# Row statistics ahead of the next projection, one root for four tiles, first weights on the sync queue

## The chip, the cores and the metric

The kernel runs on one core of a Trainium2 chip. A core has five engines that run side by side and are tied together by semaphores: TensorE (PE: matmuls, with PEld for its weight loads), VectorE (DVE), ScalarE (ACT), GpSimd (POOL) and SyncE (SP), which issues DMAs. ACT and POOL issue DMAs too. The metric is the time of one execution on the device, in microseconds (us); lower is better.

## The reference

A layer norm of x (2048 rows of 640) feeds an attention of 32 heads over cached keys and values and, beside it, a gated feed-forward network; the two outputs are multiplied and added to x.

```python
def _layernorm(x, axis=-1, eps=1e-5):
    m = jnp.mean(x, axis=axis, keepdims=True)
    v = jnp.var(x, axis=axis, keepdims=True)
    return (x - m) / jnp.sqrt(v + eps)
...
    def _A_ref(x, k_cache, v_cache, wq, wo):     # Sq = Sk = 2048, H = 32, Dh = 192
        q = (x @ wq).reshape(B, Sq, H, Dh).transpose(0, 2, 1, 3)
        scores = jnp.einsum("bhqd,bhkd->bhqk", q, k_cache) * (Dh ** -0.5)
        p = _softmax(scores, axis=-1)
        o = jnp.einsum("bhqk,bhkd->bhqd", p, v_cache)
        return o.transpose(0, 2, 1, 3).reshape(B, Sq, H * Dh) @ wo
    def _B_ref(x, w1, w3, w2):                   # F = 1536
        h = _silu(x @ w1) * (x @ w3)
        return h @ w2
    xn = _layernorm(x)
    return x + _A_ref(xn, ...) * _silu(_B_ref(xn, ...))
```

Here the transposes of the reference's lambda are written as method calls; the computation is the same.

## The kernel before

**Tiles and stages.** The 2048 rows of x are 16 tiles of 128 rows; four tiles make a query block (qb 0 to 3, 512 rows). The 2048 keys are 16 tiles, taken two at a time: a pair p, 0 to 7, is key tiles p and p + 8. A head is 4 query blocks of 8 pairs. The text writes (qb, p) for a step of head 0. After the heads come the rest of the feed-forward network and the output projection, which the change does not touch.

**A step.** `advance` (line 446) takes one step: `scores` (L374 to 387) does six half-array matmuls into a PSUM tile st2, `weights` (L391) exponentiates it on ScalarE with a bound `nb` as bias, into pT2, and `values` (L420 to 440) multiplies pT2 by the values vt into two output banks (obank, L431), in two halves of 8 matmuls. Halves are queued and done some steps later, so that TensorE has work while ScalarE exponentiates. At p = 7 `evict` (L394) adds and scales the banks on VectorE (L401 to L408). The PSUM pool ps_st has two buffers, which st2, the projections' ps and the transposes' pst share by turns.

**Projections.** `project_chunk` (L274) makes the queries of one head for one query block: matmuls of the transposed normalized rows xnT with the head's weights wq (L283 for head 0, L289 for the others, which also use xnS, a copy of xnT with its partition halves exchanged), two casts qA and qF (L291, L292; ScalarE or VectorE), and copies qS and qD by GpSimd (L295, L299). It hands back `maxima` (L303): the largest absolute values of qA and qF. With those of the keys (`key_maxima`, L315) and a sum over partitions (`bound` on GpSimd, L343; `first_bound` by a matmul, L330) they give `nb`. `finish_head` (L350) does this for a whole later head.

**Layer norm.** It is done in head 0, between the steps. `ln_stats(i)` takes mean and variance of tile i on VectorE (L184, L185); `ln_sums` does the same on ScalarE for tiles 1 and 4 (L190 to L192). `ln_root(i0)` turns two variances into two factors by a logarithm and an exponential on ScalarE (L203 to L211), and `ln_scale(i0)` scales two tiles on VectorE (L221). Tiles 0 to 7 are then turned by TensorE into a PSUM tile pst and copied to xnT (`ln_turn`, L225 to L232; `next_turn`, L234); tiles 8 to 15 are sent by transposing DMAs on SP (`ln_send`, L238, L241). `swap_rows(qb)` (L307) copies 512 columns of xnT to xnS with two DMAs issued by GpSimd.

**What sets the order.** `pin` keeps instructions in program order on their engine: nearly all of head 0 is written out by hand. The tables `posts` and `extra_at` (L493 to L516) say which layer-norm work and which projection follows or stands within which step; a step with an `extra` keeps one half of values more in the queue. A queue serves its instructions in order, so an exponential on ScalarE stands behind a root issued before it, and that root behind VectorE's statistics. At (2,2) and (3,5) the keys and the weights of head 2 are asked for. On SP the order at the start is:

```python
load_x(nc.sync, 0, 1); load_x(nc.sync, 2, 4)     # tile 1 goes on the ACT queue
# keys KA in two halves; x tiles 4 to 7; keys KB in two halves; values vt
# x tiles 8 to 11; x tiles 12 to 15
```

and the weights of head 0 go on the ACT queue (L95).

Of the kernel before, what the change touches and what calls it, by code (L numbers as in the profile page):

```python
# [16 lines left out]
P = 128  # L17
# [13 lines left out]
def _kernel_impl(ctx, tc, A_x, A_k_cache, A_v_cache, A_wq, A_wo, B_w1, B_w3, B_w2, out):  # L31
# [54 lines left out]
    def load_weights(h):  # L86
# [15 lines left out]
    def load_keys(h, mid=None):  # L102
# [5 lines left out]
        for K, c in ((KA, 0), (KB, DH - P)):  # L108
            for r in ((slice(0, HALF), slice(HALF, SK)) if h == 0 else (slice(0, SK),)):
                keep(nc.sync.dma_start_transpose(out=K[:, r], in_=kh[r, c:c + P]))  # L110
            if mid and K is KA:
                mid()
# [16 lines left out]
    with ExitStack() as actx:  # L129
# [26 lines left out]
        ASUM = {1: 0, 4: 1}  # L156
        sums = lnx.tile([P, 2], F32, name="sums")
        sqs = lnx.tile([P, 2], F32, name="sqs")
        nmean = lnx.tile([P, 2], F32, name="nmean")
# [27 lines left out]
        def ln_sums(i):  # L187
            k = slice(ASUM[i], ASUM[i] + 1)
            junk = lnp.tile([P, D], BF16, tag="junk", name="junk")
            pin(nc.scalar.activation(out=junk[:], in_=x_all[:, i, :], func=ACT.Identity, accum_out=sums[:, k]))  # L190
            pin(nc.scalar.mul(out=nmean[:, k], in_=sums[:, k], mul=-1.0 / D))
            pin(nc.scalar.activation(out=junk[:], in_=x_all[:, i, :], func=ACT.Square, bias=nmean[:, k], scale=1.0,  # L192
                                     accum_out=sqs[:, k]))
# [3 lines left out]
        def ln_root(i0):  # L197
            lv = lnp.tile([P, 2], F32, tag="lv", name="lv")
            if i0 in ASUM or i0 + 1 in ASUM:
                for t in range(2):  # L200
                    i = i0 + t
                    if i in ASUM:
                        pin(nc.scalar.activation(out=lv[:, t:t + 1], in_=sqs[:, ASUM[i]:ASUM[i] + 1], func=ACT.Ln, bias=eps_t[:],  # L203
                                                 scale=1.0 / D))
                    else:
                        pin(nc.scalar.activation(out=lv[:, t:t + 1], in_=mv[:, i, 1:2], func=ACT.Ln, bias=eps_t[:], scale=1.0))
            else:
                pin(nc.scalar.activation(out=lv[:].unsqueeze(2), in_=mv[:, i0:i0 + 2, 1:2], func=ACT.Ln, bias=eps_t[:],
                                         scale=1.0))
            rstd[i0] = lnx.tile([P, 2], F32, name=f"rstd{i0}")  # L210
            pin(nc.scalar.activation(out=rstd[i0][:], in_=lv[:], func=ACT.Exp, scale=-0.5))  # L211
# [3 lines left out]
        def ln_scale(i0):  # L215
            scaled[i0] = []
            for t in range(2):
                i = i0 + t
                xn = xnp.tile([P, D], BF16, tag="xn", name="xn")
                act = i in ASUM  # L220
                pin(nc.vector.tensor_scalar(out=xn[:], in0=x_all[:, i, :], scalar1=nmean[:, ASUM[i]:ASUM[i] + 1] if act else mv[:, i, 0:1],  # L221
                                            scalar2=rstd[i0][:, t:t + 1], op0=ALU.add if act else ALU.subtract, op1=ALU.mult))
# [22 lines left out]
        loads[0].update(load_weights(0))  # L245
# [7 lines left out]
        for copy in ln_turn(0):  # L253
            copy()
        keep_busy(2)
        for copy in ln_turn(2):
            copy()
        keep_busy(4)

# [14 lines left out]
        def project_chunk(h, qb, cast=nc.vector.tensor_copy):  # L274
# [17 lines left out]
            pin(cast(out=qF[:, qs], in_=ps[:, 512:1024]))  # L292
            keep = pin if h == 0 or h == 1 else (lambda x: x)
            for t in range(2):
                keep(nc.gpsimd.tensor_copy(out=qS[ROWS[t], qs], in_=qA[ROWS[1 - t], qs]))  # L295
            if h == 0 and qb == 0:
# [579 lines left out]
```

## Time and profile before

| | us |
|---|---|
| median of 3 runs | 1957.99 (1957.71 to 1958.47) |
| the profiled execution | 1959.34 |
| its span (first to last instruction) | 1957.3 |
| TensorE busy | 1937.9 (99%) |
| ScalarE busy | 1214.6 (62%) |
| VectorE busy | 1143.3 (58%) |
| GpSimd busy | 443.7 (23%) |

The profile page divides the span into 40 slices and gives the busy share of each engine in tenths. TensorE's row shows an 8 in the first slice and 9 from there to the last but one. Finer windows of the trace show where it is not busy: those from 0 to 100 us add up to 86.7 us of a busy TensorE, those from 100 to 300 us to 200.0.

How to read the lines: a group line gives source line, engine, operation and tiles, then total and mean duration. A waits line reads "engine line <- who ended the wait: total us, times, longest us". A timeline line begins with start and duration, and ends with the idle time in front of it and what ended it. A row of windows gives for each engine the busy time and in brackets the number of instructions, in the order PE, PEld, DVE, ACT, POOL; then the TensorE clock granted (1.00 is full), the busy share of the DMA engines and GB/s. "to landing" is the time from the issue of a DMA to its completion.

### The profile page before, as it was taken

The numbers are of one execution on the slowest core, as the hardware profiler recorded it, in microseconds if no ns is written. First come the engines' busy times: TensorE is split into PE (matmuls) and PEld (weight loads), VectorE is DVE, ScalarE is ACT, GpSimd is POOL, SyncE is SP. The second block draws the span as 40 slices with busy tenths as digits, with TensorE's granted clock in tenths as the row PEclk, the third lists the DMA queues.
The fourth block names the chain that finished last, engine by engine and source line by source line (L and its number), as shares of the span: only waits on it lengthen the run. The fifth ranks groups of instructions, "written<-read, shape, count | busy, mean of one in ns | idle before, by whom it ended". The sixth has DMA issues, their size and how long they took to land.

```text
span 1957.3 us, 60510 instructions
## 1 busy us (share of the span) xinstructions
PE 1937.9 (99%) x27230; PEld 1389.2 (71%) x27239; DVE 1143.3 (58%) x2268; ACT 1214.6 (62%) x1181; POOL 443.7 (23%) x641
## 2 busy tenths in 40 slices
PE   8899999999999999999999999999999999999998
PEld 4577777777777777777777777766666666567775
DVE  7666667666666666666666666666665655531111
ACT  5577767677777777777777777777777777210000
POOL 2522222222222222222222222222222210000000
PEclk9999999999999999999999999999999999999999
DMA  8721222223222333232223232323232203938882
GB/s 171 143 58 46 68 51 69 58 60 67 62 68 62 68 62 68 54 86 64 76 54 76 46 84 46 84 46 84 47 60 49 60 10 109 270 76 139 154 154 53
DMA packets 358314, 154.83 MB, mean 79 GB/s; under 512 B 309200, under 2 KB 351152, under 8 KB 358048
## 3 DMA queue, kind: packets, MB, share of 16 engines
q1 hardware_dynamic: 342576, 119.13, 28.4%
q0 software_dynamic: 8832, 26.55, 5.6%
q10 hardware_dynamic: 6640, 5.21, 1.1%
q8 instruction: 215, 3.52, 0.8%
q14 instruction: 51, 0.42, 0.1%
HBM read 56.23 MB, written 31.98 MB: 45 GB/s over the span
## 4 chain that ended last, share of the span: by engine, by line
PE 96%; DVE 1%; DMA 1%; ACT 1%; SPq 0%; POOL 0%; issue 0%; ACTq 0%; DVEq 0%
PE obank L431 34%; PE st L385 33%; PE ps L289 14%; PE ps_s L695 11%; PE ps_f L716 3%; PE ps_gu L566 1%; DMA wq<-in_A_wq_dram 1%; PE ps L591 0%; PE ps L283 0%; DMA vt<-in_A_v_cache_dram 0%; SPq L110 0%; ACT pT L391 0%; DVE st L303 0%; DVE st L184 0%; DMA x_all<-in_A_x_dram 0%
## 5 line engine op out<-in xcount | busy, mean ns | idle before, releaser
L391 ACT ACTIVATE pT<-st,nb 128x1024 bf16<-128x1024 f32 x1016 | 1131.9, 1115 | 446.4 <-PE st L385 443.3
L431 PEld LDWEIGHTS <-pT 64*128 64x128 bf16 x16384 | 747.2, 94 | 214.7 <-ACT pT L391 5.1
L431 PE MATMUL obank<-vt,pT 64*128 64x193 bf16 x16384 | 869.7, 243 | 5.2 <-ACT pT L391 4.7
L401 DVE COPY osum<-obank 128x386 f32<-128x386 f32 x256 | 142.5, 557 | 502.5 <-PE obank L431 502.4
L385 PE MATMUL st<-qA,KA 64*128 64x512 bf16 x2048 | 406.9, 377 | 1.0 <-ACT pT L391 0.6
L385 PE MATMUL st<-qS,KC 64*128 64x512 bf16 x1024 | 385.5, 376 | 0.0
L385 PE MATMUL st<-qF,KB 64*128 64x512 bf16 x1024 | 385.5, 376 | 0.0
L385 PE MATMUL st<-qD,KC 64*128 64x512 bf16 x1024 | 385.5, 376 | 0.0
L385 PE MATMUL st<-qS,KB 64*128 64x512 bf16 x1024 | 385.5, 376 | 0.0
L295 POOL COPY qS<-qA 64x512 bf16<-64x512 bf16 x256 | 193.0, 754 | 608.4 <-DVE qA L291 574.1
L289 PE MATMUL ps<-xnT,wq 64*128 64x512 bf16 x1240 | 291.8, 378 | 2.5 <-ACT pT L391 2.5
L289 PE MATMUL ps<-xnS,wq 64*128 64x512 bf16 x1240 | 286.4, 378 | 0.9 <-DMA wq<-in_A_wq_dram 0.9
L385 PEld LDWEIGHTS <-KC 64*128 64x128 bf16 x2048 | 192.7, 94 | 104.4 <-issue 1.1
L289 PEld LDWEIGHTS <-wq 64*128 64x128 bf16 x2480 | 139.4, 94 | 105.4 <-DMA wq<-in_B_w_dram 3.8
L695 PE MATMUL ps_s<-wo_sb,oT 128*128 128x320 bf16 (+2 forms) x1535 | 208.8, 299 | 0.1
L385 PEld LDWEIGHTS <-KB 64*128 64x128 bf16 x2048 | 192.8, 94 | 13.4 <-issue 0.4
L695 PEld LDWEIGHTS <-oT 128*128 128x128 bf16 x1536 | 148.3, 98 | 60.5
L408 DVE TENSOR_TENSOR ostage<-osum,rl_all 128x384 bf16<-128x384 f32 x256 | 150.5, 588 | 8.8
L402 DVE TENSOR_TENSOR osum<-osum,obank 128x386 f32<-128x386 f32 x256 | 142.7, 557 | 8.9
L385 PEld LDWEIGHTS <-KA 64*128 64x128 bf16 x2048 | 118.6, 94 | 16.2 <-issue 3.1
L700 DVE SCALAR_TENSOR_TENSOR tmp<-ps_s,g_all 128x320 f32<-128x320 f32 (+2 forms) x32 | 15.6, 488 | 176.0 <-PE ps_s L695 176.0
L99 POOL DMA_DIRECT2D wq<-in_A_wq_dram x62 | 45.8, 738 | 278.0 <-PE ps L289 265.8
(99 smaller groups left out, 1237.4 us busy)
## 6 DMA issues: line engine op xcount, KB each, us to landing
vt<-in_A_v_cache_dram SPq DMA_DIRECT2D x32, 768.0 KB, 6.3
o_scr<-ostage SPq DMA_DIRECT2D x64, 384.0 KB, 3.0
wo_sb<-in_A_wo_dram POOLq DMA_DIRECT2D x1, 7680.0 KB, 31.3
wq<-in_A_wq_dram POOLq DMA_DIRECT2D x31, 160.0 KB, 3.0
hT_scr<-hblk SPq DMA_DIRECT2D x16, 256.0 KB, 3.0
xnS<-xnT POOLq DMA_DIRECT2D x8, 320.0 KB, 4.6
xt<-in_A_x_dram POOLq DMA_DIRECT2D x16, 160.0 KB, 9.3
wq<-in_B_w_dram POOLq DMA_DIRECT2D x31, 80.0 KB, 2.7
```

Of the source, the lines that this page charges most:

```text
L99: keep(nc.gpsimd.dma_start(out=wq[ROWS[t], :, c0:c1], in_=w.rearrange("(s p) d -> p s d", p=DT)))
L289: pin(nc.tensor.matmul(ps[:, t * 512:(t + 1) * 512], lhsT=wq[ROWS[t], s, :], rhs=xs[ROWS[t], s // 2, qs], start=(s == 0), stop=(s == 2 * D ...
L295: keep(nc.gpsimd.tensor_copy(out=qS[ROWS[t], qs], in_=qA[ROWS[1 - t], qs]))
L385: pin(nc.tensor.matmul(st2[:, t * 512:(t + 1) * 512], lhsT=k[ROWS[t], ks], rhs=q[ROWS[t], qs], start=(s == 0), stop=(s == 2)))
L391: pin(nc.scalar.activation(out=pT2[:], in_=st2[:], func=ACT.Exp, scale=SCALE, bias=nb[:]))
L401: pin(nc.vector.tensor_copy(out=osum[:], in_=ov[:, 0, :, 0:DH + 1]))
L402: pin(nc.vector.tensor_tensor(out=osum[:], in0=osum[:], in1=ov[:, 1, :, 0:DH + 1], op=ALU.add))
L408: pin(nc.vector.tensor_tensor(out=ostage[:, b * 2:b * 2 + 2, hg * DH:(hg + 1) * DH], in0=osum[:, :, 0:DH], in1=rl.unsqueeze(2).to_broadcas ...
L431: pin(nc.tensor.matmul(acc["o"][b][:, r, (j % 2) * 256:(j % 2) * 256 + DH + 1], lhsT=pT2[ROWS[r], t * 512 + j * P:t * 512 + (j + 1) * P], ...
L566: pin(nc.tensor.matmul(ps[:, o:o + 512], lhsT=w_sb[:, c, (fl - 1) * P:fl * P], rhs=xnT[:, c, qs], start=(c == 0), stop=(c == DC - 1)))
L695: pin(nc.tensor.matmul(ps, lhsT=oT[:, k, :], rhs=wo_sb[:, k, c0:c1], start=(k == 0), stop=(k == OC - 1)))
L716: pin(nc.tensor.matmul(ps[:, pi * 512:pi * 512 + c1 - c0], lhsT=lhs[fc], rhs=w2_sb[:, fc, c0:c1], start=(fc == 0), stop=(fc == FC - 1)))
```

## The change

Six things change, all in head 0 and before it; the steps of heads 1 to 31 are the same.

1. The weights of head 0 are loaded from the SP queue, between the keys KA and KB, instead of from the ACT queue.
2. x tiles 4 to 7 go in two loads of two tiles: 4 and 5 behind KB, 6 and 7 behind vt.
3. `ln_sums` stays for tile 1 alone; tile 4 goes to VectorE. Tiles 4 and 5 are normalized after the first scores, not before them, and the turns of tiles 4 to 7 move from (0,1) and (0,3) to (0,3) and (0,4), each with one copy by ScalarE and one by VectorE. The projection of block 1 moves from (0,4) to (0,5).
4. `ln_root` can serve four tiles; it does so for tiles 8 to 11 and 12 to 15, and their statistics stand in front of the projection of the next block.
5. The first key maxima are taken over all keys at once, and the first query maxima are read from PSUM instead of from the casts.
6. Key maxima and query maxima of head 1 get fixed places; its bound is asked for at (3,6); the weights of head 2 are loaded at (2,2) instead of (3,5).

```diff
             for w, t, c0, c1 in parts:
-                pin(nc.scalar.dma_start(out=wq[:, t, :, c0:c1], in_=w.rearrange("(c p) d -> p c d", p=P)))
+                pin(nc.sync.dma_start(out=wq[:, t, :, c0:c1], in_=w.rearrange("(c p) d -> p c d", p=P)))
...
-        loads[0] = load_keys(0, lambda: load_x(nc.sync, 4, 8))
+        first_w = {}
+        loads[0] = load_keys(0, [lambda: first_w.update(load_weights(0)), lambda: load_x(nc.sync, 4, 6)])
+        loads[0].update(first_w)
         copy_keys(loads[0])
+        load_x(nc.sync, 6, 8)
         load_x(nc.sync, 8, 12)
...
-        def ln_root(i0):
-            lv = lnp.tile([P, 2], F32, tag="lv", name="lv")
...
+        def ln_root(i0, n=2):
+            lv = lnp.tile([P, n], F32, tag=f"lv{n}", name="lv")
+            if i0 == 0:
+                pin(nc.scalar.activation(out=lv[:, 0:1], in_=mv[:, 0, 1:2], func=ACT.Ln, bias=eps_t[:], scale=1.0))
+                pin(nc.scalar.activation(out=lv[:, 1:2], in_=sqs[:], func=ACT.Ln, bias=eps_t[:], scale=1.0 / D))
             else:
-                pin(nc.scalar.activation(out=lv[:].unsqueeze(2), in_=mv[:, i0:i0 + 2, 1:2], func=ACT.Ln, bias=eps_t[:],
+                pin(nc.scalar.activation(out=lv[:].unsqueeze(2), in_=mv[:, i0:i0 + n, 1:2], func=ACT.Ln, bias=eps_t[:],
...
         def next_turn(i0):
-            for copy in ln_turn(i0, (nc.vector.tensor_copy, nc.vector.tensor_copy)):
+            for copy in ln_turn(i0, (nc.scalar.copy, nc.vector.tensor_copy)):
                 copy()
...
-                for col, (src, r0) in ((2, (qA, 0)), (3, (qF, PGW))):
-                    pin(nc.vector.tensor_reduce(out=st[r0:P, col, qb:qb + 1], in_=src[r0:P, qs], axis=AX.X, op=ALU.max,
+                for col, src, r0 in ((2, ps[:, 0:512] if first else qA[:, qs], 0),
+                                     (3, ps[:, 512:1024] if first else qF[:, qs], PGW)):
+                    pin(nc.vector.tensor_reduce(out=st[r0:P, col, qb:qb + 1], in_=src[r0:P, :], axis=AX.X, op=ALU.max,
...
         def first_product():
             hd = heads[0]
-            pin(nc.vector.tensor_tensor(out=hd["st"][:, 0:2, 0], in0=hd["st"][:, 0:2, 0], in1=hd["st"][:, 0:2, 1], op=ALU.max))
...
         start_head(0)
-        ln_sums(4)
-        for k in range(2):
-            key_maxima(0, 0, k, 2)
-        ln_stats(5)
-        ln_root(4)
         for k in range(2):
-            key_maxima(0, 1, k, 2)
+            key_maxima(0, k)
         maxima = project_chunk(0, 0, nc.scalar.copy)
+        maxima()
         loads[1] = load_weights(1)
         swap_rows(0)
-        maxima()
...
-        ln_scale(4)
...
         posts = {
-            (0, 0): ((ln_stats, 6),),
-            (0, 1): ((ln_stats, 7), (ln_root, 6), (ln_scale, 6)),
-            (0, 4): ((ln_stats, 8),),
-            (0, 5): ((ln_stats, 9), (ln_root, 8), (swap_rows, 1)),
-            (0, 6): ((ln_send, 8), (ln_stats, 10)),
-            (0, 7): ((ln_stats, 11), (ln_root, 10), (ln_send, 10)),
+            (0, 0): ((ln_stats, 4), (ln_stats, 5)),
+            (0, 1): ((ln_root, 4), (ln_stats, 6), (ln_scale, 4)),
+            (0, 2): ((ln_stats, 7),),
+            (0, 3): ((ln_root, 6), (ln_scale, 6), (ln_stats, 8)),
+            (0, 4): ((ln_stats, 9), (ln_stats, 10), (ln_stats, 11)),
+            (0, 5): ((ln_root, 8, 4), (ln_send, 8), (swap_rows, 1)),
+            (0, 6): ((ln_send, 10),),
             (1, 2): ((ln_stats, 12), (ln_stats, 13)),
-            (1, 4): ((ln_root, 12), (ln_send, 12)),
-            (1, 5): ((ln_stats, 14), (ln_stats, 15), (swap_rows, 2)),
-            (1, 6): ((ln_root, 14), (ln_send, 14)),
+            (1, 3): ((ln_stats, 14), (ln_stats, 15)),
+            (1, 4): ((ln_root, 12, 4), (ln_send, 12), (ln_send, 14)),
+            (1, 5): ((swap_rows, 2),),
             (2, 5): ((swap_rows, 3),),
         }
         extra_at = {
-            (0, 1): ((next_turn, 4),),
-            (0, 3): ((next_turn, 6),),
-            (0, 4): ((first_project, 0, 1),),
+            (0, 3): ((next_turn, 4),),
+            (0, 4): ((next_turn, 6),),
+            (0, 5): ((first_project, 0, 1),),
...
+        behind_at = ((2, 2), (2, 6), (3, 3), (3, 6))
+        key_at = ((2, 2), (2, 3), (2, 5), (2, 6), (3, 2), (3, 3), (3, 4), (3, 5))
...
-                if (qb, p) in ((2, 3), (2, 7), (3, 3), (3, 6)):
+                if (qb, p) in behind_at:
                     behind.pop(0)()
...
                 if (qb, p) == (2, 2):
                     copy_keys(heads[1]["L"])
-                    loads[2] = load_keys(2)
+                    loads[2] = {**load_weights(2), **load_keys(2)}
                 if (qb, p) == (3, 5):
-                    loads[2].update(load_weights(2))
                     copy_keys(loads[2])
-                if qb >= NQB - 2 and p > 3 or qb == NQB - 1 and p > 1:
-                    if key_slots:
-                        key_maxima(1, *key_slots.pop(0))
-            if not more:
-                while key_slots:
+                if (qb, p) in key_at:
                     key_maxima(1, *key_slots.pop(0))
-                finish_head(1)
+                if (qb, p) == (3, 6):
+                    finish_head(1)
```

`load_keys` takes a list of two calls in place of one and makes one behind each of KA and KB. The remaining lines of the diff follow from these: `rstd` is kept by tile, the sums have one column, and the four copies to xnT at the start are written behind both turns, as they stood on ScalarE before.

More of the change, by code (lines that the diff above doesn't have):

```diff
@@ L195, in _kernel_impl @@
+            pin(nc.scalar.mul(out=nmean[:], in_=sums[:], mul=-1.0 / D))
+            pin(nc.scalar.activation(out=junk[:], in_=x_all[:, i, :], func=ACT.Square, bias=nmean[:], scale=1.0,
+                                     accum_out=sqs[:]))
         rstd = {}
-        def ln_root(i0):
-            lv = lnp.tile([P, 2], F32, tag="lv", name="lv")
[L199 to L206, printed above, removed]
+        def ln_root(i0, n=2):
[3 more added lines that the diff above has]
+                pin(nc.scalar.activation(out=lv[:, 1:2], in_=sqs[:], func=ACT.Ln, bias=eps_t[:], scale=1.0 / D))
@@ L213, in _kernel_impl @@
+            pin(nc.scalar.activation(out=r[:], in_=lv[:], func=ACT.Exp, scale=-0.5))
+            for t in range(n):
+                rstd[i0 + t] = r[:, t:t + 1]
         scaled = {}
```

42 lines of the change are left out of this document (17 added, 25 removed).

## The prediction

> **What bounds the kernel now.** I read the chain of waits first, then who waited for whom on TensorE and ScalarE, then the granted clock, then the order of time around each wait, and last the DMA issues of the sync queue (SP). Times are us from the span's start; (q,p) is pair p of query block q of head 0.
>
> ```profile
> PE 96%; DVE 1%; DMA 1%; ACT 1%; SPq 0%; POOL 0%; issue 0%; ACTq 0%; DVEq 0%
> ```
>
> The end hangs on TensorE, so only time in which TensorE stands still, or runs slowly, can be won. TensorE's waits between 20 and 100, and the moments of the long ones:
>
> ```profile
> PE obank L431 <- ACT pT L391: 4.7, 2, 2.6
> PE ps L289 <- ACT pT L391: 2.5, 1, 2.5
> PE ps L289 <- DMA wq<-in_A_wq_dram: 0.9, 1, 0.9
> PE obank L431 <- DVE osum L402: 0.5, 1, 0.5
> ...
> 32.58 0.29 ACT L208 ACTIVATE lv<-mv,eps_t 128x2 f32<-128x2 f32 x1 [3.17 <-DVE mv L185]
> 34.16 0.82 PE L431 MATMUL obank<-vt,pT 64*128 64x193 bf16 x8 [2.62 <-ACT pT L391]
> 54.40 0.60 PE L431 MATMUL obank<-vt,pT 64*128 64x193 bf16 x8 [2.04 <-ACT pT L391]
> 88.71 0.70 POOL L343 PARTITION_ALL_REDUCE nb<-ns  x1
> 90.61 0.37 PE L289 MATMUL ps<-xnT,wq 64*128 64x512 bf16 x1 [2.46 <-ACT pT L391]
> 91.86 0.39 PE L289 MATMUL ps<-xnS,wq 64*128 64x512 bf16 x2 [0.88 <-DMA wq<-in_A_wq_dram]
> ```
>
> The reader is to see three holes. At 34.16 (A) and 54.40 (B) TensorE waits for an exponential that stands on ScalarE behind a root (L208), and the root waits for row statistics that VectorE does only after the casts and maxima of a projection. At 90.61 (C) the exponential waits for head 1's bound (L343), which stood on GpSimd behind three weight issues and two key copies; then head 2's weights are late too. A fourth hole (D, 0.5) waits for an eviction. Behind each of the first three the clock is halved:
>
> ```profile
> 34.30:37.50 3.20, 3.20 (x32) 2.28 (x30) 2.41 (x8) 2.27 (x4) 0.00 (x0) 0.50 0.96 179
> 54.80:58.00 3.20, 3.20 (x24) 1.54 (x20) 2.82 (x6) 1.67 (x2) 0.00 (x0) 0.50 1.54 149
> 92.30:95.50 3.20, 3.20 (x18) 1.45 (x16) 0.00 (x0) 1.19 (x2) 0.93 (x2) 0.50 1.18 237
> ```
>
> (Third column from the right: the clock.) The slow spells last about 3.4, so each costs 1.7. A costs 2.62 + 1.7 = 4.3, B 3.7, C 2.46 + 0.88 + 1.7 = 5.0, D 0.5: 13.5 in all. The other views that decide are the sync queue's:
>
> ```profile
> 33.62 6.06 SPq L241 DMA_TRANSPOSE xnT<-xn  x4
> 39.73 2.62 SPq L110 DMA_TRANSPOSE KA<-in_A_k_cache_dram  x1
> 50.42 8.59 SPq L241 DMA_TRANSPOSE xnT<-xn  x4
> 59.06 2.67 SPq L110 DMA_TRANSPOSE KA<-in_A_k_cache_dram  x1
> DMA to landing us min/median/max: 2.6/3.9/7.7
> ```
>
> These are the transposes of normalized rows 1024-1535 and 1536-2047 (the last line is of all eight), which the projections at 44.67 and 63.60 need.
>
> **Startup.** The first weights leave the ACT queue for SP, between the halves KA and KB; 320 KB of x go behind KB and 320 KB behind the values (vt). Before KB 320 KB fewer are queued, and KB landed at 12.6 and 13.4 before. The weights' second part held TensorE 0.24; ahead of KB it no longer should. ScalarE loses the second tile's sums (11.01 to 13.8). Ten matmuls from 11.20 then end at about 13.5, and the cast of qA starts at 13.55 instead of 13.97. The maxima from PSUM still wait for the cast of qF (the built program has this wait), end at 14.62, and cost 2 x 0.69, as the cast from PSUM by VectorE does (0.69 for 512 columns); one combining step (0.2) is gone. The first exponential comes at 16.75 instead of 17.27: +0.5. Bounds: the key reductions are no longer cut in two and start only when all of KB is there; if that is at 13.0 they end at 15.4 and I lose 0.2. No gain is above 0.7, since the copies to xnT at 11.15 are unchanged.
>
> **Block 0.** Stats go ahead of the projection, so root 8 no longer follows its casts; two turns by TensorE move to (0,3) and (0,4), each with a ScalarE copy (0.62) in place of a VectorE one. TensorE's work from the third scores at 18.2 to the scores of (1,2): 8 scores x 0.65, 15 half values x 0.33, 2 turns x 0.72, projections 2.33 and 2.16 = 16.1. Behind it I find small waits of 1.35: 0.6 at the turns, where pst waits for exp and scaling, and 0.7 at (0,7), where three stats in a row (3.2) put the casts of the projection 0.9 late. Sum 35.7, against 40.63 before: +4.9. From there to the projection of rows 1024-1535 are 4.04 (44.67 - 40.63), so TensorE is ready for it at 39.7.
>
> **What is late next.** This projection needs four transposes. They are issued when the four scalings (4 x 0.44) behind one root of four are done, from 32.1; at the same time the bound of block 1 releases the swap (L310, two DMAs of 320 KB by GpSimd). Before, the swap was issued at 31.13 and the last transpose landed at 38.45 + 2.6 = 41.05; in the second burst 50.77 and 56.93 + 3.73 = 60.66. Both are 9.9 from the swap's issue to the last landing. So the transposes land at 32.1 + 9.9 = 42.0. Bounds: 38.7 if the swap did not disturb (four issues 1.3 apart, 2.6 to land), 46.3 if the last takes the longest landing (38.6 + 7.7). I take 42.0, the row both bursts gave. TensorE waits 2.3, and its clock may fall (1.7).
>
> The second burst stands on SP behind head 1's keys and values, and those behind the first burst. Before, from last landing to last landing it took 60.66 - 41.05 = 19.6, with queues nearly always filled. The scalings come earlier now (about 6 behind the first landing, 9.4 before) but the bytes in the queue are the same, and the second swap now falls into the values' transfer. So 42.0 + 19.6 = 61.6 at most, 42.0 + 11.1 (values landed, 52.17 before) + 4 x 1.3 = 58.3 at least; I take 61.0, near the upper end, because the swap's 640 KB pass in this stretch either way. TensorE is ready at 42.0 + 15.2 (before, 18.93 less hole B) + 1.7 = 58.9 and waits 2.1. The projection starts 63.60 - 61.0 = 2.6 earlier than before, and one slow spell behind the wait takes 1.7: 0.9 is left. So the 13.5 shrink to what lies behind this point, since the transposes are now what ends last: removing A and B moves the wait, it does not shorten the transfer chain.
>
> The Trainium skill, "TensorE: Matmul & The Clock Gate", Why this matters for your kernels, says to keep idle gaps of TensorE under about 3 us, since one idle window halves the clock. The trace halves it behind a gap of 2.04 (hole B), so the measurement decides here. By the Trainium skill's figure neither new wait would be punished, and the sum would be 1.7 better, about 1949.9.
>
> **Behind it.** Key maxima and query maxima are spread, so VectorE is done with them 0.5 before the eviction at (2,7): D goes, +0.5 (0 to 0.5). Head 2's weights are issued at (2,2), and the bound is asked for at (3,6). GpSimd then has copies until 84.2, one issue of head 3's weights that the build puts ahead of them (0.74, mostly behind the cast), two key copies, a memset: 84.3 + 2.1 + 0.3, and the bound ends at 87.4, where the scores of head 1 are ready at 87.8. The cover is 0.4; if it is gone, the wait is back at a price of one for one. C goes: +5.0. What heads 2 to 31 issue stands in the same order as before.
>
> Sum: 0.9 + 0.5 + 5.0 = 6.4. The profiled run took 1959.34, 2.0 over its span of 1957.3, and lies 1.35 above the median of the runs, 1957.99. 1959.34 - 6.4 - 1.35 = **1951.6**.
>
> **Rivals.**
> - *The transposes come in time* (0.20). The first lands by 39.7 and the second by its need. For: alone they take 1.3 each; DMA had gaps of about 1 us. Against: 7.7 next to the swap. Then 4.9 + 3.7 + 0.5 + 5.0 = 14.1: 1943.9.
> - *No slow spell behind the waits* (0.08): the wait before the last rows stays under about 2 (it is 2.1 by the sum), and waits of 0.5 and 0.7 left the clock whole. 1951.6 - 1.7 = 1949.9. The Trainium skill's rule above is this rival.
> - *The bound of head 1 stays late* (0.15): GpSimd still serves copies ahead of it, and only the weights' 0.88 is won. For: the cover is 0.4 and GpSimd spans are rough. Then 0.9 + 0.5 + 0.9 = 2.3: 1955.7.
> - *Slower* (0.10): the four transposes land one behind another at 7.7 each, all at the swap's mercy. 32.1 + 31 = 63.1 for the first burst, 82.7 for the second, 19.1 later than before: 1957.99 + 19.1 + 1.7 - 5.5 = 1973. It is slower from a second landing at about 67.4. For: the 7.7 landing. Against: in that burst the next two landed 0.6 apart, overlapped.
>
> **How the numbers follow.** Forecast 0.47, its own range 1947.5 (second landing 58.3) to 1953.5 (first landing 1 to 2 later). The range 1943.5 to 1957 takes in all but the slower case and odds and ends. Faster by over 0.2% (3.9; about what a measurement can tell from no change) is forecast, the first two rivals and little else: 0.74. Within: 0.15. Slower: 0.11.
>
> **What would show it.** Right: no L208-type root in front of a late exponential; the projection of rows 1024-1535 waiting for DMA xnT until near 42, that of the last rows until near 61; no wait for nb at head 1; slow spells only behind the xnT waits. Wrong: those projections start without a wait (then 1944), or head 1 still waits for nb.

## The result and the profile after

The changed kernel took 1949.41 us at the median of six runs (1948.17 to 1950.25), the kernel before 1958.23 beside it (1957.29 to 1959.34): a ratio of 0.9954, interval 0.9941 to 0.9967. That is 8.8 us faster; 6.4 were forecast, 1951.6. The profiled execution took 1949.38, with a span of 1947.6, so it stands for the median.

The chain of waits of the changed kernel, shares by engine, in which ScalarE's 1% is gone:

```profile
PE 97%; DVE 1%; DMA 1%; SPq 0%; POOL 0%; ACT 0%; issue 0%; DVEq 0%; POOLq 0%
```

TensorE's two longest groups of waits in the changed kernel between 20 and 100 (total, times, longest):

```profile
PE ps L279 <- DMA xnT<-xn: 5.0, 2, 2.7
PE ps L285 <- ACT pT L388: 0.4, 1, 0.4
```

The long ones in TensorE's timeline (start, duration, and in brackets the wait and what ended it):

```profile
41.44 2.32 PE L279 MATMUL ps<-xnT,wq 128*128 128x512 bf16 x10 [2.30 <-DMA xnT<-xn]
59.20 1.02 PE L279 MATMUL ps<-xnT,wq 128*128 128x512 bf16 x4 [2.66 <-DMA xnT<-xn]
```

All waits for a late exponential (A, B), for head 1's bound and head 2's weights (C) and for the eviction (D) are gone but for 0.4. In their place TensorE waits 5.0 for transposed rows, at the two projections where the forecast put it.

The SP queue's timeline shows what is waited for: four transposes from 31.22 and four from 47.18, and between them head 1's keys and values.

```profile
31.22 8.35 SPq L237 DMA_TRANSPOSE xnT<-xn  x4
39.62 2.65 SPq L110 DMA_TRANSPOSE KA<-in_A_k_cache_dram  x1
...
47.18 9.02 SPq L237 DMA_TRANSPOSE xnT<-xn  x4
```

The first burst's last landing is at 41.20, the second's at 59.11. The clock stayed whole, which these windows of the changed kernel show (third column from the right; each window is 3.413 long; in all traces here the granted clock changes only at multiples of that):

```profile
37.18:40.60 3.42, 1.96 (x34) 1.57 (x29) 2.88 (x10) 2.74 (x5) 0.70 (x2) 1.00 1.09 123
40.60:44.01 3.41, 2.57 (x14) 1.11 (x16) 0.21 (x1) 0.14 (x1) 0.00 (x0) 1.00 0.82 156
54.25:57.66 3.41, 2.29 (x36) 1.42 (x32) 1.71 (x3) 2.71 (x3) 3.23 (x6) 1.00 1.22 137
57.66:61.08 3.42, 1.88 (x9) 0.91 (x10) 0.00 (x0) 0.00 (x0) 1.96 (x3) 1.00 1.06 230
```

Where the time came from is best read at the same four exponentials of ScalarE in each trace. Starts in us:

| kernel | first | (2,6) | head 1, (0,4) | from there to the end |
|---|---|---|---|---|
| before | 17.27 | 68.44 | 99.57 | 1857.7 |
| changed | 16.56 | 64.02 | 89.55 | 1858.0 |

The rest takes the same time, so all is decided before 100. Of the 10.0 between the two profiled executions 0.7 come at the start, 3.7 up to (2,6), and 5.6 behind it. (The median moved by 8.8: the profiled execution before lay above its median.)

### The profile page after: what moved, and what is told of

It reads as the page before. It is cut to its first block, busy times and chain, and to the rows that moved or that the text cites. A ratio compares the mean times of both kernels' runs of the same rounds, so it can differ in the third digit from the quotient of the medians.

```text
span 1947.6 us, 60514 instructions
## 1 busy us (share of the span) xinstructions
PE 1933.0 (99%) x27239; PEld 1322.8 (68%) x27239; DVE 1139.6 (59%) x2266; ACT 1212.4 (62%) x1173; POOL 441.9 (23%) x641
## 4 chain that ended last, share of the span: by engine, by line
PE 97%; DVE 1%; DMA 1%; SPq 0%; POOL 0%; ACT 0%; issue 0%; DVEq 0%; POOLq 0%
PE obank L428 35%; PE st L382 33%; PE ps L285 14%; PE ps_s L684 11%; PE ps_f L705 3%; PE ps_gu L555 1%; DMA xnT<-xn 0%; PE ps L580 0%; SPq L110 0%; PE ps L279 0%; DMA KB<-in_A_k_cache_dram 0%; DVE st L186 0%; ACT pT L388 0%; DVE st L301 0%; DVE st L313 0%
## 5 line engine op out<-in xcount | busy, mean ns | idle before, releaser
L428 PEld LDWEIGHTS <-pT 64*128 64x128 bf16 x16384 | 715.4, 94 | 240.2 <-ACT pT L388 0.8
L428 PE MATMUL obank<-vt,pT 64*128 64x193 bf16 x16384 | 853.0, 243 | 0.1
L382 PE MATMUL st<-qA,KA 64*128 64x512 bf16 x2048 | 390.7, 376 | 0.5 <-ACT qA L287 0.2
L285 PEld LDWEIGHTS <-wq 64*128 64x128 bf16 x2480 | 122.1, 94 | 115.3 <-issue 0.6
L382 PEld LDWEIGHTS <-KA 64*128 64x128 bf16 x2048 | 103.1, 93 | 17.4 <-issue 2.3
```

The source lines that it names most:

```text
L285: pin(nc.tensor.matmul(ps[:, t * 512:(t + 1) * 512], lhsT=wq[ROWS[t], s, :], rhs=xs[ROWS[t], s // 2, qs], start=(s == 0), stop=(s == 2 * D ...
L382: pin(nc.tensor.matmul(st2[:, t * 512:(t + 1) * 512], lhsT=k[ROWS[t], ks], rhs=q[ROWS[t], qs], start=(s == 0), stop=(s == 2)))
L428: pin(nc.tensor.matmul(acc["o"][b][:, r, (j % 2) * 256:(j % 2) * 256 + DH + 1], lhsT=pT2[ROWS[r], t * 512 + j * P:t * 512 + (j + 1) * P], ...
```

## The experiments

Each kernel ran beside the kernel before. The base is the changed kernel unless a row says otherwise; the last three columns are from one profiled execution.

| kernel | median us | runs | ratio to before | TensorE's waits, 20 to 100 | (2,6) | head 1, (0,4) |
|---|---|---|---|---|---|---|
| changed | 1949.41 | 6 | 0.9954 [0.9941, 0.9967] | xnT 5.0 | 64.02 | 89.55 |
| swaps late | 1950.06 | 5 | 0.9946 [0.9933, 0.9960] | xnS 4.5 | 59.85 | 92.36 |
| keys late | 1955.25 | 11 | 0.9986 [0.9977, 0.9995] | xnT 4.3, qF 2.5 | 66.40 | 92.05 |
| both late | 1953.51 | 8 | 0.9977 [0.9966, 0.9988] | qF 6.3 | 66.60 | 93.66 |
| pairs | 1952.63 | 6 | 0.9966 [0.9954, 0.9979] | pT 5.0 | 68.07 | 93.61 |
| before, head 1's part alone | 1953.62 | 10 | 0.9974 [0.9965, 0.9984] | pT 4.7 | 68.39 | 93.91 |
| swaps spread | 1949.82 | 5 | 0.9954 [0.9941, 0.9968] | xnT 4.9 | 66.37 | 91.89 |
| swaps on SP | 1945.23 | 5 | 0.9930 [0.9917, 0.9944] | xnT 1.5 | 60.56 | 86.09 |
| before, filled | 1955.88 | 11 | 0.9987 [0.9978, 0.9996] | see below | 66.79 | 95.96 |
| swaps on SP, values late | 1943.71 | 5 | 0.9925 [0.9911, 0.9939] | 0.6 in all | 59.45 | 84.97 |
| swaps on SP, pairs | 1951.54 | 5 | 0.9965 [0.9951, 0.9979] | pT 5.0 | 66.79 | 92.33 |
| old start | 1948.96 | 4 | 0.9953 [0.9938, 0.9968] | xnT 4.1 | 64.82 | 90.34 |

**What makes the transposes late.** First the swaps were moved away from them:

```diff
-            (0, 5): ((ln_root, 8, 4), (ln_send, 8), (swap_rows, 1)),
+            (0, 5): ((ln_root, 8, 4), (ln_send, 8)),
...
+            (1, 1): ((swap_rows, 1),),
...
-            (1, 5): ((swap_rows, 2),),
+            (2, 1): ((swap_rows, 2),),
```

> The two swaps (L308) of rows 512-1023 and 1024-1535 leave the stretch of the transposes: they move from (0,5) to (1,1) and from (1,5) to (2,1). All else as in the changed kernel (1949.4). Theory (the swap is what makes the transposes late: three of the four issues of the first burst took 2.0 to 2.6 beside it where the first took 1.24): four issues of about 1.3 from 31.2, last landing near 39, so TensorE no longer waits at the projection of rows 1024-1535 (wait 0 to 0.3 instead of 2.3). The second burst is issued 2.3 earlier (near 44.9) behind head 1's values, lands near 54 instead of 59.1, and its wait falls from 2.7 to under 1. Time 1944.4 to 1946. Rival one (the transposes are slow by themselves or behind what SP has queued, not by the swap): both waits stay within 0.5 of 2.3 and 2.7, time 1949 to 1950. Rival two (only the first burst suffers from the swap; the second is held by head 1's keys and values in front of it): first wait gone, second grows to 4 to 5, time 1948.5 to 1949.5. The swaps are later too: if they come too late for the projections of head 1, TensorE waits there for xnS instead.

The first burst in the SP queue's timeline:

```profile
32.03 5.20 SPq L237 DMA_TRANSPOSE xnT<-xn  x4
```

And TensorE's one long wait in its timeline:

```profile
74.85 0.61 PE L285 MATMUL ps<-xnS,wq 64*128 64x512 bf16 x2 [4.51 <-DMA xnS<-xnT]
```

Without the swap beside it the first burst is issued in 5.20 instead of 8.35, and each of its four lands 2.6 behind its issue, the last at 38.58: 38.7 was the forecast's lower bound "if the swap did not disturb". Both waits for xnT are gone, and (2,6) comes 4.2 earlier than in the changed kernel. The mechanism of the theory holds. But the median is no better: the last swap (62.02) now runs beside head 2's keys and weights and lands only at 74.81, TensorE waits 4.51 for it, and from 72.65, still within the wait, two windows run at half clock. The gain went into a new wait, the last clause of the expectation. The median (1950.06) hides runs from 1945.79 to 1952.15; the profiled one was the slowest.

Second, head 1's keys and values were moved behind the second burst, and third, both edits were made together:

```diff
-                if (qb, p) == (0, 7):
-                    loads[1].update(load_keys(1))
+                if (qb, p) == (1, 5):
+                    heads[1]['L'].update(load_keys(1))
```

> Head 1's keys and values (KA, KB, vt: L110, L114) move from (0,7) to (1,5), so they stand on SP behind the second burst of transposes instead of before it. The swaps stay. Theory (the swap is the first burst's trouble, keys and values add to the second's): first wait unchanged, 2.0 to 2.6; second burst as the first one, last landing about 9.9 behind the swap's issue at 47.5, so 57.4, and its wait 0.5 to 1.5 instead of 2.7; time 1947.2 to 1948.2. Rival (the swap alone decides both): second landing stays near 59.1, wait 2.5 to 3, time 1949 to 1950. Rival (the chain behind SP's queue decides alone): second burst lands by 54, no second wait, time 1946.7. Head 1's key copies (L119) come at (2,2) and may wait for the later keys; if the keys land after 62 GpSimd is late with them.

> Both edits together: swaps at (1,1) and (2,1), head 1's keys and values at (1,5). Theory: neither burst has anything beside it, four issues 1.3 apart and 2.6 to land; TensorE waits for xnT nowhere (0 to 0.5 in all); time 1949.4 - 5.0 = 1944.4 (1944 to 1945.5). If the swap is what matters alone, the same as with the late swaps alone. If neither matters, 1949 to 1950. If a wait of 2 or more remains at either place, a third cause holds the bursts (the issue order on SP or the time of the scalings).

With the keys late alone the second burst landed at 58.80 instead of 59.11, against 57.4 by the theory: beside the swap it makes little difference what stood ahead. With both edits no wait for xnT was left, as expected. Yet both kernels are slower than the changed one, for a reason that I had not reckoned with. VectorE's timeline with both edits:

```profile
62.98 0.68 DVE L313 TENSOR_REDUCE st<-KB 64x1 f32<-64x512 bf16 x1 [4.89 <-DMA KB<-in_A_k_cache_dram]
63.70 0.69 DVE L287 CAST qA<-ps 128x512 bf16<-128x512 f32 x1
```

The key maxima of head 1 stand in VectorE's queue in front of the casts of the last projection. They waited for the late keys (4.89 for KB, and 4.64 for KA before), the casts waited behind them, and TensorE 6.3 for qF. I had taken GpSimd's key copies for the keys' first reader; it is these maxima. With the keys late alone the profiled execution (1951.75) was the fastest of 11, so it doesn't show what the others lost beyond its 2.5 for qF. Their mean granted clock gives a hint: 0.997 to 0.999 against 1.000 there, where one halved window takes some 0.0009 off the mean (half of 3.413 in 1950). So slow spells are probably much of it.

Fourth, the first swap stayed at (1,1), and the two last ones were set apart from head 2's weights, at (2,0) and (2,2).

```diff
-            (0, 5): ((ln_root, 8, 4), (ln_send, 8), (swap_rows, 1)),
+            (0, 5): ((ln_root, 8, 4), (ln_send, 8)),
...
+            (1, 1): ((swap_rows, 1),),
...
-            (1, 5): ((swap_rows, 2),),
-            (2, 5): ((swap_rows, 3),),
+            (2, 0): ((swap_rows, 2),),
+            (2, 2): ((swap_rows, 3),),
```

> The late swaps once more, but the last two set apart from head 2's weights: swap of rows 512-1023 at (1,1), of 1024-1535 at (2,0), of 1536-2047 at (2,2), ahead of head 1's key copies and head 2's weights. With the late swaps alone both waits for xnT were gone, and a wait of 4.5 for the last swap (issued at 62.0 beside head 2's keys and weights, landed at 74.8) with two halved windows (3.4) took their place. Theory (the price of the swap moves with it; it is free only where nothing that is needed soon lies beside it): no wait for xnT, last swap issued near 56, landed by 68, before the projection that needs it near 75; waits of 1 or less in all between 30 and 90; time 1944.4 (1943.5 to 1946), whole clock. Rival (any place between 38 and 75 hits some transfer that ends last): a wait of 1.5 to 5 for xnS, xnT or wq appears, time 1947 to 1951; the trace names which.

This missed. GpSimd's timeline shows why:

```profile
44.78 0.59 POOL L340 PARTITION_ALL_REDUCE nb<-ns  x1 [0.45 <-DVE ns L337]
45.36 1.37 POOL L308 DMA_DIRECT2D xnS<-xnT  x2
```

And the SP queue's what came of it:

```profile
45.30 11.03 SPq L237 DMA_TRANSPOSE xnT<-xn  x4
```

A place in the program is only a place in GpSimd's queue. Nothing that waits stood between the bound of block 2 and the swap, so it was issued at 45.36, straight beside the second burst, whose issues took 11.03; TensorE waited 4.89 at the last rows. Against my intention the swap was back beside the burst, with the values still under way, and so was the wait: this too speaks for the swap as the cause.

Fifth, the swaps were put where nothing can run beside the bursts, in line behind them on SP:

```diff
-        def swap_rows(qb):
+        def swap_rows(qb, eng=nc.sync):
...
-                pin(nc.gpsimd.dma_start(out=xnS[ROWS[t], :, qs], in_=xnT[ROWS[1 - t], :, qs]))
+                pin(eng.dma_start(out=xnS[ROWS[t], :, qs], in_=xnT[ROWS[1 - t], :, qs]))
...
-        swap_rows(0)
+        swap_rows(0, nc.gpsimd)
...
-            (0, 5): ((ln_root, 8, 4), (ln_send, 8), (swap_rows, 1)),
-            (0, 6): ((ln_send, 10),),
+            (0, 5): ((ln_root, 8, 4), (ln_send, 8)),
+            (0, 6): ((ln_send, 10), (swap_rows, 1)),
...
-            (1, 5): ((swap_rows, 2),),
-            (2, 5): ((swap_rows, 3),),
+            (1, 5): ((swap_rows, 2), (swap_rows, 3)),
```

> All swaps but the first are issued by SP instead of GpSimd, in line behind the transposes: swap of rows 512-1023 behind the first burst, those of 1024-1535 and 1536-2047 behind the second, before head 2's keys. Nothing of the swap can run beside the bursts then. Theory: first burst lands near 39 as with the late swaps (issues 1.3 apart), second near 55; no wait for xnT; head 1's and head 2's keys come some 2 to 4 later, which nothing needs so early; time 1944 to 1946, whole clock. Rival (it was GpSimd's queue, not the bytes: swaps on SP slow what stands behind them as much): the second burst lands at 58 or later and its wait is 1.5 to 3, time 1946.5 to 1949.

The first burst landed at 37.82, the second at 55.61; 1945.23, as expected, but with a wait of 1.52 left at the second, which was issued while the values were still arriving. So the values were moved behind the second burst too (`load_vt` is called at (1,5) for head 1):

> The kernel with the swaps on SP (1945.2, one wait of 1.52 left before the last rows), and head 1's values (vt) moved on SP from before the second burst to behind it. There the second burst was issued at 45.9 while the values (45.2 to 52.0) were under way, its first landing at 52.6, its last at 55.6. Theory (what is left of the second wait is the transfer ahead in the queue): four issues of 1.2 to 1.3 from about 45, last landing near 52.5, no wait for xnT (0 to 0.2), time 1945.2 - 1.5 = 1943.7 (1943.2 to 1944.5). Rival (the keys ahead of the values hold the burst just as much): first landing still at 50 or later, last at 54 or later, wait 0.5 to 1.5, time 1944.4 to 1945.3. The values are needed by head 1 near 80; if they are late TensorE waits for vt there.

Both bursts in the SP queue's timeline of this kernel:

```profile
31.71 5.20 SPq L239 DMA_TRANSPOSE xnT<-xn  x4
...
45.36 6.19 SPq L239 DMA_TRANSPOSE xnT<-xn  x4
```

And TensorE's longest wait between 20 and 100, to which 0.2 for another exponential come:

```profile
PE ps L287 <- ACT pT L390: 0.4, 1, 0.4
```

The second burst landed at 52.91, no wait for xnT is left, and the time is 1943.71 (1943.46 to 1944.63; 1943.7 expected). This version beats both kernels: its runs lie 3.5 or more under the lowest of the changed kernel. What decided the two waits is thus shown: the swap's transfer beside the transposes for the larger part, the values ahead of the second burst for the last 1.5. What stands behind the swap on SP pays instead: the issue of KA took 4.19 there, 2.65 in the changed kernel, but nothing needs KA so early.

The Trainium skill, "DMA: Bandwidth & Descriptors", § Queues, rings and completion order, states that each DMA engine takes its queues in turn, packet by packet. That would be how a swap on GpSimd's queue takes its share from a burst on SP's, and why it does not when it stands behind the burst on the same queue. The runs agree in the outcome (issue of four 8.35 beside, 5.20 without); that the turns of the single packets are the reason is not shown here.

**What the early statistics and the grouping are worth.** The statistics of tiles 9 to 11, 14 and 15 were put back behind the casts, and a root for each pair:

```diff
-            (0, 4): ((ln_stats, 9), (ln_stats, 10), (ln_stats, 11)),
-            (0, 5): ((ln_root, 8, 4), (ln_send, 8), (swap_rows, 1)),
-            (0, 6): ((ln_send, 10),),
+            (0, 5): ((ln_stats, 9), (ln_root, 8), (swap_rows, 1)),
+            (0, 6): ((ln_send, 8), (ln_stats, 10)),
+            (0, 7): ((ln_stats, 11), (ln_root, 10), (ln_send, 10)),
...
-            (1, 3): ((ln_stats, 14), (ln_stats, 15)),
-            (1, 4): ((ln_root, 12, 4), (ln_send, 12), (ln_send, 14)),
-            (1, 5): ((swap_rows, 2),),
+            (1, 4): ((ln_root, 12), (ln_send, 12)),
+            (1, 5): ((ln_stats, 14), (ln_stats, 15), (swap_rows, 2)),
+            (1, 6): ((ln_root, 14), (ln_send, 14)),
```

> The grouping is undone alone: statistics 9 to 11 and 14, 15 stand behind the casts again and each pair of tiles has its own root, as before the change; startup, the two turns' places, head 1's bound and all the rest as in the changed kernel. Theory (the waits trade places): ScalarE's root at (0,5) and (1,5) makes exponentials late again, TensorE waits 2.0 to 2.7 for pT at each, and then the transposes, issued later still, cost it less than the 2.3 and 2.7 of now, because it arrives later; the sum of the waits stays within 1.5 of 5.0. The time is then 1949 to 1951 if the clock stays whole, and 1951 to 1954 if one or both of the waits halve it as in the profile before (1.7 each). Rival (the grouping is what brought the gain): both kinds of wait in full, 9 to 10 us of waits, time 1953.5 to 1957. Rival (the grouping does nothing): no wait for pT, time 1949 to 1950.

TensorE's long waits in its timeline:

```profile
33.79 0.51 PE L428 MATMUL obank<-vt,pT 64*128 64x193 bf16 x8 [2.95 <-ACT pT L388]
54.03 0.51 PE L428 MATMUL obank<-vt,pT 64*128 64x193 bf16 x8 [2.04 <-ACT pT L388]
```

The windows behind them, at half clock:

```profile
34.67:38.09 3.42, 3.42 (x34) 2.30 (x30) 2.73 (x7) 1.96 (x5) 0.00 (x0) 0.50 1.02 189
55.15:58.57 3.42, 3.42 (x26) 1.50 (x22) 3.22 (x8) 1.11 (x1) 0.00 (x0) 0.50 1.17 93
```

A and B are back with 2.95 and 2.04, and no wait for xnT is left: 5.0 of waits against 5.0 in the changed kernel. The waits traded places, as the theory had it. What is left between the two profiles, 4.05 at (2,6), is 0.7 from the start of this execution and the two halved windows, 3.4. The same edit was made on the kernel with the swaps on SP, where the transposes are out of the way:

> The kernel with the swaps on SP (1945.2), with the grouping undone again: statistics 9 to 11 and 14, 15 behind the casts, a root for each pair. Theory (the waits only traded places in the changed kernel, because the transposes came next; with the transposes out of the way the grouping is worth its full price): TensorE waits for pT 2.5 and 2.0 at about 31 and 51, both behind a root, each halving the next window (1.7) if it falls within one; the transposes then cost nothing. Time 1945.2 - 1.5 + 4.5 + 3.4 = 1951.6 (1948.2 with a whole clock, to 1952.2). Rival (the grouping is worth little by itself): 1945 to 1947.

Here it costs 6.3 (1951.54 against 1945.23), as the 1951.6 of the expectation has it, though in the profiled execution by another path: both halved windows belong to A (2.95), the first from 32.12, within that wait, and none to B (2.04). The early statistics and the grouped root are worth a wait only where what comes next is not late as well. Both were undone together, so which of the two brings how much isn't shown.

**What head 1's part is worth.** On the kernel before, only the part for head 1 was changed (weights of head 2 at (2,2), fixed places for the maxima, the bound asked for at (3,6)).

> The kernel before with one part of the change alone: head 2's weights issued at (2,2), head 1's maxima spread, its bound asked for at (3,6). Startup, statistics, roots, transposes and swaps as before. Theory (hole C is the late bound of head 1 and costs 2.46 + 0.88 of waits, plus 1.7 of halved clock where a window of 3.413 holds over 2 us of idle; hole D 0.5): holes A and B stay as they are, C and D shrink to about 0.4; time 1958.6 less 3.4 to 5.5, so 1953.1 to 1955.2, and no slow spell near 92. Rival (the bound stays late behind GpSimd's copies): only the 0.88 of the weights is won, 1957 to 1958. Rival (the changed kernel's block 0, which comes earlier, is what makes the bound come in time): the wait for nb is over 1.5 here.

TensorE's longest group of waits:

```profile
PE obank L431 <- ACT pT L391: 4.7, 2, 2.6
```

A and B stand as before, C and D are down to 0.4, and no window near 92 is halved. From (2,6) to head 1, (0,4) the trace takes 25.52, before 31.13: 5.6, all that the changed kernel gains there. At the median it is 5.0 (1953.62 against 1958.64 beside it).

**What the clock costs.** In the kernel before, 16 matmuls of zeros by ones were added into an open accumulator in front of the matmuls that wait at A and B:

```diff
+                if hd["h"] == 0 and (qb, p, ts[0], bs[0]) in ((0, 6, 0, 0), (1, 7, 0, 0)):
+                    for _ in range(16):
+                        pin(nc.tensor.matmul(acc["o"][0][:, 0, 0:DH + 1], lhsT=zeros_w[:], rhs=ones_w[:, 0:DH + 1],
+                                             start=False, stop=False))
```

> The kernel before, with 16 matmuls of a zero matrix by 193 columns (about 0.083 each, 1.3 in all) added to an open accumulator right in front of the two values matmuls that wait at holes A and B; they add zero. They run inside the waits, so the waits keep their length and only their idle time falls, from 2.62 and 2.04 to 1.3 and 0.7. Theory (the clock is halved for one window of about 3.4 behind a window that is idle for over some 1.9 to 2.0): no slow spell behind A and B any more, though both values matmuls start at 34.2 and 54.4 as before; 3.4 faster than before, 1955 to 1955.6; the spell behind C (not filled) stays, unless the window's edge falls so that it splits the wait. Rival (the spells have another cause, or fillers are paid in full): same time as before or up to 2.7 slower, 1958 to 1961.5.

The fillers and the waiting matmul behind them at A, in TensorE's timeline:

```profile
32.30 1.51 PE L430 MATMUL obank<-ones_w,zeros_w 128*128 128x193 bf16 x16
34.99 0.51 PE L437 MATMUL obank<-vt,pT 64*128 64x193 bf16 x8 [1.18 <-ACT pT L393]
```

The window in which the wait at A ends:

```profile
33.59:37.00 3.41, 2.23 (x37) 1.50 (x36) 2.76 (x8) 2.48 (x5) 0.00 (x0) 1.00 0.99 191
```

More work made the kernel faster, by 2.8 at the median (3.4 expected): the waits end as late as before, and the clock stays whole behind A and B. But the profiled execution alone would not show that the fillers did it. Its window edges, at 33.59 and 54.07, cut both waits (A's into 1.22 and 1.40, B's into 1.66 and 0.37, with the fillers' time counted as wait), which by the rule of the last section leaves the clock whole even without them. What speaks for the fillers is all the runs: the mean granted clock was 0.999 or 1.000 in each of the eleven, and 0.997 or 0.998 in fourteen of the twenty of the kernel before beside them. So a halved window is a price of its own. In this execution the clock stayed whole behind C too, although C was not filled: the edge at 88.20 cut its waits, so that the windows on its two sides hold 1.70 and 1.36 of idle time (their length less TensorE's busy time). (The start of this execution was 0.8 later than in the profile before, 18.09 for the first exponential; KB landed at 14.11 there, 13.43 before.)

**What the start is worth.** The three edits of the startup were undone: the weights back on the ACT queue, x tiles 4 to 7 in one load ahead of KB, the maxima from the casts. The rest of the start stayed as changed, the reduction over all keys at once among it.

> The changed kernel with the startup undone: first weights on the ACT queue, x rows 512-1023 in one transfer ahead of KB, query maxima from the casts instead of PSUM. All else as changed. Theory: the startup brought 0.7: first exponential near 17.3 instead of 16.6 and everything behind it 0.5 to 0.7 later, TensorE's wait at the first weights (0.24) back; the waits of 2.3 and 2.7 may shrink by as much, if the transposes depend on the DMA queues and not on TensorE, so the time is between 1949.4 and 1950.2. Rival (x rows behind the keys make the statistics late): statistics or scalings of tiles 4 to 7 now come earlier, and the time is 1948.5 to 1949.2.

The first exponential came at 18.25, not near 17.3: KB landed at 13.76 instead of 12.09, and the key reduction in one piece (2.28) begins only then. So the startup's edits depend on each other, and undoing them costs 1.7 at the first exponential of these two executions. At head 1, (0,4) 0.8 of it is left, because TensorE then waits 4.1 instead of 5.0 for the transposes (the profile names 2.99 of it "issue", but the last transpose landed at 43.72 and the projection started at 43.81). The medians, 1948.96 and 1949.41, don't differ measurably; 1949.4 to 1950.2 were expected. The median lies in the rival's range (1948.5 to 1949.2), but the rival's reason is not seen: the statistics and scalings come no earlier here, the four scalings ahead of the first transposes start at 32.43 instead of 30.75, as much later as the first exponential.

## Why the prediction was right, step by step

- *Startup, 0.5.* The first exponential came at 16.56 (16.75 forecast), 0.7 earlier. The chain that ends last there starts with KB: it landed at 12.09 (12.6 and 13.4 for its halves before), its reduction took 2.28, the maxima 1.40. The mechanism is right: KB landed whole at 11.80 to 12.91 in the nine profiled kernels with this startup, at 13.12 to 14.11 in the four with the old loads. The size is less sure: the same nine have the first exponential at 16.41 to 17.38, the kernel before and the one with head 1's part alone at 17.27 and 17.34.
- *Block 0, 4.9.* Hole A is gone; TensorE was ready for the projection of rows 1024 to 1535 at 41.44 - 2.30 = 39.1 (39.7 forecast). Right.
- *What is late next.* The transposes, as named. First burst: last landing 41.20 (42.0 forecast), wait 2.30 (2.3 forecast). That the wait agrees to the digit is luck: TensorE came 0.6 earlier than forecast and the landing 0.8. The experiments confirm the lower bound's reasoning (38.7 without the swap): without it the last transpose lands at 37.8 to 38.6. Nothing here tests the upper bound.
- *The second burst* is the term that was mis-sized. The distance between the two last landings was 60.66 - 41.05 = 19.6 before; the forecast took 19.0, so 61.0. It was 59.11 - 41.20 = 17.9, and the landing came 1.9 earlier than forecast, 0.8 of it from the first burst and 1.1 from this distance. I kept nearly the old distance because the bytes in the queue are the same; but the burst was issued 3.2 earlier than before (47.18 against 50.42), and half of that came through. Nor is the 9.9 from the swap's issue to the last landing a constant: it was 9.75 in the first burst and 11.6 in the second (59.11 - 47.53).
- *The slow spell behind the waits, 1.7,* did not come in the profiled execution. This is the step that failed, and the rival "no slow spell" (0.08) had the right outcome for the wrong reason: it asked for a wait under 2, and the waits were 2.30 and 2.66. What decides is the idle time within one window, as the last section shows; that the edges cut both waits in this execution is luck. With these two terms, 1.9 + 1.7, the 0.9 of the last rows' projection becomes 4.5; it started 63.60 - 59.20 = 4.4 earlier. Whether the other five runs had a slow spell their mean clocks (0.998 to 1.000) don't tell.
- *D 0.5 and C 5.0.* 5.6 behind (2,6), and 5.6 with this part alone. Right in size. But the cover of 0.4 for head 1's bound was not there. ScalarE waited 0.95 for it in the changed kernel, and 0.4 of that reached TensorE. The second line is from the kernel before, TensorE's last matmul of the scores that this exponential reads:

```profile
82.26 2.12 ACT L388 ACTIVATE pT<-st,nb 128x1024 bf16<-128x1024 f32 x2 [0.95 <-POOL nb L340]
86.13 0.38 PE L385 MATMUL st<-qF,KB 64*128 64x512 bf16 x1
```

Head 1's first scores are thus ready at 86.5, 0.9 ahead of the bound that the forecast has at 87.4; the 87.8 that it took are the second scores. And since 0.4 of waiting stayed, what was removed was worth some 0.5 more than its terms (5.6 + 0.4 against 5.5); what that is stays open.

- *Rivals.* The transposes in time (1943.9) is what the kernel with swaps and values in line on SP does: 1943.71. The change itself did not bring it. The bound staying late is ruled out by the trace (0.4), the slower case too: landings overlapped as in the bursts before.
- *The sum.* 0.9 + 0.5 + 5.0 = 6.4 was forecast against the profiled execution; with 4.4 in place of 0.9 it is 9.9, and the two profiled executions differ by 1959.34 - 1949.38 = 10.0.

## What to carry to other kernels

Removing a wait shows what was hidden behind it: before counting the gain, ask when the next operand lands and what is in flight beside it. A transfer that nobody needs soon should stand on the same queue behind the one that is needed next, since a later place in another engine's program is no later time if that engine is idle. A short wait of TensorE can cost nearly its own length again in clock, so fill it or remove it whole.

## What was not expected of the hardware

**The clock goes by fixed windows.** In every trace here the granted clock changes only at multiples of 3.413 from a start that differs from one execution to the next (full clock first granted at 4.38 to 7.38). Counting idle time of TensorE within each such window between 20 and 100, over all profiles, every window with 2.04 or more was followed by one at half clock (2.04 three times, then 2.14 to 3.27, fourteen in all). With 1.85 or less a window at full clock was never followed by one at half (1.85, 1.83 and 1.70 are the largest); only once, with the pairs on top of the swaps on SP, did a window that was itself at half clock and idle for 0.81 leave the next one at half too. The same wait of 2.04 (B) was punished in the kernel before and not in that other kernel, since there the edge at 52.60 cut it. The windows at B of the kernel before:

```profile
51.27:54.69 3.42, 1.38 (x26) 0.80 (x22) 2.25 (x7) 1.84 (x4) 0.88 (x2) 1.00 0.88 185
54.69:58.10 3.41, 3.41 (x28) 1.74 (x24) 2.92 (x6) 1.78 (x2) 0.00 (x0) 0.50 1.49 149
```

And of the kernel with the pairs on top of the swaps on SP:

```profile
52.60:56.01 3.41, 1.58 (x26) 1.11 (x28) 2.01 (x5) 2.89 (x5) 0.00 (x0) 1.00 0.56 109
56.01:59.43 3.42, 3.42 (x48) 2.00 (x46) 3.23 (x9) 2.04 (x4) 0.59 (x1) 1.00 0.80 99
```

First column of numbers after the window's length: TensorE's busy time, 1.38 (idle 2.04) and 1.58 (idle 1.83); the row behind shows 0.50 and 1.00. In the changed kernel the edges at 40.60 and 57.66 cut both waits, so that no window had more than 1.54. Another execution may have its edges elsewhere, so 1.7 more or less from run to run is to be expected of these kernels. Most timed runs have no trace, but their mean granted clock agrees: of the 48 runs of the kernel before beside the experiments, the 26 with 0.997 took 1958.25 to 1960.67, the five with 1.000 1954.48 to 1956.34. The Trainium skill, "TensorE: Matmul & The Clock Gate", § What's actually happening, states a free-running window of 3413 ns, and the traces agree. Its § Why this matters for your kernels, which allows gaps up to about 3 us, is too generous here: about 2 us within one window were enough.

**A transposing DMA is slow already at its issue.** Alone the issue holds SP for 1.2 and the landing follows 2.6 behind it; beside a swap of two times 320 KB the issue takes 2.0 to 2.6 in the changed kernel and the landing up to 8.7. It need not be a swap: with the swaps late, the second burst's first issue took 2.92 and landed 6.77 behind it, with the values still under way. The delay thus moves down SP's queue to whatever stands behind.
